# First expert layer: 320 slots per expert in blocks of 128, 128 and 64, where there were 336 in blocks of 128, 128 and 80

## The chip, the cores and the metric

The kernel runs on one core of a Trainium2 chip. The metric is the device time of one launch in microseconds (us). Engines are named as in the profile: PE (TensorE, matmuls), PEld (its weight loads), DVE (VectorE), ACT (ScalarE), POOL (GpSimd) and SP (SyncE, which here only issues transfers).

## The reference

Three layers stand behind each other: attention with a bias from running sums, a layer of eight experts with the two best per token, and a layer of eight experts in which every token goes to every expert. The first expert layer is the one that is changed:

```python
N, D, E, F = (1152, 512, 8, 1024)
logits = x @ w_gate
noisy_logits = logits + np.log1p(np.exp(x @ w_noise)) * noise
top2 = np.argpartition(-noisy_logits, 2, axis=1)[:, :2]
...
for e in range(E):
    for k in range(2):
        mask = top2[:, k] == e
        h = np.maximum(x[mask] @ w1[e], 0.0)
        out[mask] += top2_w[mask, k, None] * (h @ w2[e])
```

So 2304 pairs of token and expert are spread over eight experts, 288 for each on average. For the inputs of the reference its routing gives the experts 273, 287, 288, 283, 286, 286, 297 and 304 tokens.

## The kernel before

**Number format.** Values that go to PE are split in two fp16 parts, a high part and the rest (`hi`, `lo`; `hh`, `hl` for the hidden layer). A product is three matmuls: high by high, high by low, low by high.

**Order.** Each engine has its own queue, in order; the kernel schedules by hand, so the order of the code is the order of each queue. Steps on different engines wait for each other only through the data and buffers that they share.

**Attention** (to about 136 us) also issues, between its steps (`between`), work for what follows: the weights of the first expert (`w_load`) and `zero_rows`, which clears the first C0 rows of every expert's place in the DRAM tensor `xs_d`. There are two such transfers per expert, of C0/2 rows each, all from a small tile `z` of zeros, through SP's queue. SP's queue also carries the attention's loads, its transposes (`dma_start_transpose`) and a small transfer of row maxima per step (`rt` to `xq`, L246), for which PE waits in the next step.

**Routing** (`route`, `scatter`, `order`) finds the two best experts of each token, gives each token a slot in its experts, and writes the tokens' two parts to these slots of `xs_d` by indirect transfers of POOL (L826). The writes overlap the cleared rows, so they wait for the zeros. Expert 0's tokens are not read from DRAM: 72 matmuls with 0/1 matrices `hot0` of C0 columns select them (L971), and eight copies (L1011, L1013) put them in SBUF. Then comes a branch (L1016): if any expert has more than C0 tokens, `general()` computes the whole layer in fp32 for all tokens.

**First expert layer**, experts e = 0 to 7 one after the other. `fetch` brings the tokens of the next expert with a transposing transfer. For each of 8 slices f of the hidden layer there are 12 matmuls with C0 moving columns (L1051 to L1053); ACT makes the high part (L1054) and the full value in PSUM (L1055), and DVE subtracts (L1056). Then the slots go through w2 in blocks of up to 128 slots, which are the stationary side; the moving side has 512 columns. A block is 8 x 3 matmuls (L1070 to L1072); ACT copies the result out (L1074), and POOL, or SP for expert 7, issues its transfer to `y_d` (L1076). The weights of the next expert are split between these steps (`w_conv`): ACT makes the high part (L551), DVE the low part (L552), and then the next chunk is loaded into the buffer. Up to four chunks are in flight; from expert 7's weights on (`LAST`) two.

Beside expert 7, `lower` gathers each token's result of the lower of its two experts from `y_d` (L960, POOL) and adds it (L1026, DVE, one per slice f). After expert 7 the results of the other expert are gathered and added (L1125), and the sums, transposed on PE or by transfers (L1108), are the input of the second expert layer, which takes the rest of the time.

The block loop of the kernel before:

```python
BL = [(b, min(128, C0 - b)) for b in range(0, C0, 128)]
...
for b, n in BL:
    ps = bank()
    o = ps[0:n, :]
```

Of the kernel before, what the change touches and what calls it, by code (L numbers as in the profile page):

```python
# [438 lines left out]
SW1 = 16.0  # L439
SH2 = SX2 * SW1  # L440
CAP = 1152
C0 = 336
LAG = 2
NST = 2
NW = 8
# [10 lines left out]
def attention_moe_moe_kernel(  # L456
# [40 lines left out]
    def bank():  # L497
        return psum.tile([128, 512], F32, name="ps", tag="b")
# [156 lines left out]
    def zero_rows(i, z):  # L655
        if i == 0:
            nc.gpsimd.memset(z, 0.0)
        r0 = i // 2 * CAP + i % 2 * (C0 // 2)
        nc.sync.dma_start(out=xs_d[r0:r0 + C0 // 2, :].rearrange("(p r) (a c) -> p (r a) c", p=56, a=2),
                          in_=z.unsqueeze(1).to_broadcast([56, C0 // 56, D]))  # L660

    xhl_p = ctx.enter_context(tc.tile_pool(name="xhl", bufs=1))
    xall = xhl_p.tile([128, NT * 2 * D], F16, name="xall")
# [252 lines left out]
    with ExitStack() as actx:  # L916
        r_p = actx.enter_context(tc.tile_pool(name="r", bufs=1))

        z = r_p.tile([56, D], F16, name="z")

        gates_in = gate_weights()

        def between(it):
            if it == -4:
                constants()
            if 1 <= it < 7:
                next(gates_in)
            if it == 6:
                gate_split()
            if 12 <= it < 16:  # L930
                w_load(0, it - 11)
            if 8 <= it < 8 + E:
                zero_rows(2 * it - 16, z)
                zero_rows(2 * it - 15, z)
            if it == 9:
                first.append(route(r_p, 0, 4, False))
            if 13 <= it < 15:
                turn2(it - 13)
            if it == 16:
                gate_part()  # L940
                turn2(2)
            if it >= 9:
                next(first[0], None)

        attention(tc, actx, psum, q, k, v, s, xhl, scat, between, idle)
# [18 lines left out]
    with ExitStack() as m1:  # L964
# [69 lines left out]
        def fetch(e):  # L1034
            XT[e] = e_p.tile([128, 2 * KD, C0], F16, name="xsT")
            nc.sync.dma_start_transpose(out=XT[e], in_=xs_d[e * CAP:e * CAP + C0, :])

        BL = [(b, min(128, C0 - b)) for b in range(0, C0, 128)]
        for e in range(E):
            if 0 < e < E - 1:  # L1040
                fetch(e + 1)
            w_load(e + 1)
            xt = XT.pop(e)
            hh, hl = [e_p.tile([128, KF, C0], F16, name=f"h{u}") for u in "hl"]
            for f in range(KF):
                ps = bank()
                o = ps[:, 0:C0]
                fs = slice(f * 128, (f + 1) * 128)
                for c in range(KD):
                    wh, wl = [W[e, 0][u][:, c, fs] for u in range(2)]  # L1050
                    nc.tensor.matmul(out=o, lhsT=wh, rhs=xt[:, c, :], start=(c == 0), stop=False)  # L1051
                    nc.tensor.matmul(out=o, lhsT=wh, rhs=xt[:, KD + c, :], start=False, stop=False)  # L1052
                    nc.tensor.matmul(out=o, lhsT=wl, rhs=xt[:, c, :], start=False, stop=(c == KD - 1))  # L1053
                nc.scalar.activation(out=hh[:, f, :], in_=o, func=AF.Relu, scale=SH / (SX * SW))  # L1054
                nc.scalar.activation(out=o, in_=o, func=AF.Relu, scale=SH / (SX * SW))  # L1055
                nc.vector.tensor_tensor(out=hl[:, f, :], in0=o, in1=hh[:, f, :], op=OP.subtract)  # L1056
                if f % 2 or e == 0:
                    w_conv(e + 1)
                if e == 0 and f == FETCH:
                    fetch(1)  # L1060
                if e == E - 1:
                    next(lows)
            w2h, w2l = [t.rearrange("p c (a d) -> p (c a) d", a=2) for t in W[e, 1]]
            if e == E - 1:
                w_conv(E, False)
            for b, n in BL:
                ps = bank()
                o = ps[0:n, :]
                for f in range(KF):
                    nc.tensor.matmul(out=o, lhsT=hh[:, f, b:b + n], rhs=w2h[:, f, :], start=(f == 0), stop=False)  # L1070
                    nc.tensor.matmul(out=o, lhsT=hh[:, f, b:b + n], rhs=w2l[:, f, :], start=False, stop=False)  # L1071
                    nc.tensor.matmul(out=o, lhsT=hl[:, f, b:b + n], rhs=w2h[:, f, :], start=False, stop=(f == KF - 1))  # L1072
                y = e_p.tile([128, D], F32, name="y", bufs=3)
                nc.scalar.activation(out=y[0:n], in_=o, func=AF.Copy, scale=1.0 / (SH * SW))  # L1074
                eng = nc.gpsimd if e + 1 < E else nc.sync
                eng.dma_start(out=y_d[e * C0 + b:e * C0 + b + n, :], in_=y[0:n])  # L1076
                if e == E - 1 and b < 256:
                    ups.append(gather(b // 128, 1, e * C0 + b + 128))
                if e < E - 1 or b:
                    w_conv(e + 1, e + 1 < E)  # L1080
                next(lows, None)
            if e + 1 < E:
                w_conv(e + 1)
            if e == E - 2:
                lows = lower()
                next(lows)
# [340 lines left out]
```

## Time and profile before

| What | Value |
|---|---|
| median of 3 runs | 1158.96 us (1158.96 to 1161.39) |
| the profiled execution: time | 1163.45 us |
| the profiled execution: span | 1161.7 us |
| PE busy | 1086.6 us, 94% of the span |
| DVE, ACT, POOL busy | 51%, 43%, 21% |
| mean granted clock of PE | 0.968 of full speed |

The span runs from the first to the last instruction. Matmuls are pipelined: their "mean ns" is the time through the pipeline, so the cost of one is read from the distance between the starts of two. The granted clock is a share of full speed: 1.00 is 2.4 GHz, 0.50 is 1.2 GHz.

### The profile page before, as it was taken

What the parts mean: (1) busy time and instruction counts of PE and PEld (TensorE: products, weight loads), DVE (VectorE), ACT (ScalarE), POOL (GpSimd) and SP (SyncE); (2) the same over time, 40 slices, a digit from 0 to 9 for tenths busy, and PEclk for the clock granted to TensorE, in tenths of its full rate; (3) what the DMA queues carried; (4) which work ended last, traced back from release to release, by engine and by line L of the source; (5) the groups of instructions that cost most, each with busy time, mean ns of one, the idle gap of its engine ahead of it and who ended that gap; (6) DMA issues with size and microseconds to landing.
All of it is one profiled execution on the core that took longest, in us unless ns stands there. A gap on an engine that the chain in (4) does not pass through costs nothing.

```text
span 1161.7 us, 18353 instructions
## 1 busy us (share of the span) xinstructions
PE 1086.6 (94%) x7450; PEld 670.2 (58%) x7450; DVE 597.4 (51%) x1099; ACT 496.9 (43%) x926; POOL 242.9 (21%) x317
## 2 busy tenths in 40 slices
PE   4988739999999978999999999999999999999996
PEld 3566625555555557566666666566566566566553
DVE  8997745444444555755454444454454354354231
ACT  5786715555555433344443443343343343343220
POOL 6674570000000340441220220220220220220000
PEclk8798978999999998999999999999999999999998
DMA  5668666666654744021021021021021022010001
GB/s 99 126 119 153 201 219 178 202 190 191 191 191 155 223 125 128 19 73 55 19 73 55 19 73 55 19 73 56 19 71 58 19 64 65 19 55 1 10 28 46
DMA packets 134766, 108.41 MB, mean 93 GB/s; under 512 B 74546, under 2 KB 108642, under 8 KB 134674
## 3 DMA queue, kind: packets, MB, share of 16 engines
q1 hardware_dynamic: 130226, 92.90, 29.0%
q0 software_dynamic: 4448, 14.26, 3.5%
q8 instruction: 60, 0.98, 0.4%
q14 instruction: 32, 0.26, 0.1%
HBM read 79.03 MB, written 18.09 MB: 84 GB/s over the span
## 4 chain that ended last, share of the span: by engine, by line
PE 76%; DMA 2%; DVE 2%; issue 1%; ACT 1%; POOL 1%; SPq 0%; POOLq 0%; DVEq 0%; ACTq 0%
PE ps L1324 31%; PE ps L1266 24%; PE ps L1117 3%; PE ps L1071 3%; PE ps L1072 3%; PE ps L1070 3%; PE ps L1051 3%; PE ps L1052 3%; PE ps L1053 3%; DMA wst<-in_moe_w_dram 1%; DMA yg<-y_d,idy 1%; DVE wp L552 1%; ACT wp L551 1%; DVE hop L1238 0%; DMA y_d<-y 0%
## 5 line engine op out<-in xcount | busy, mean ns | idle before, releaser
L1324 PE MATMUL ps<-wp,hop 128*128 128x512 f16 x1536 | 366.6, 379 | 0.2 <-PE ps L1195 0.2
L1266 PEld LDWEIGHTS <-wp 128*128 128x128 f16 x2352 | 230.1, 98 | 101.2 <-issue 1.6
L1324 PEld LDWEIGHTS <-hop 128*128 128x128 f16 x1536 | 150.2, 98 | 141.6 <-issue 0.3
L552 DVE SCALAR_TENSOR_TENSOR wp<-wst,wp 128x1024 f16<-128x1024 f32 (+1 forms) x153 | 178.7, 1187 | 102.3 <-ACT wp L551 101.7
L1266 PE MATMUL ps<-xall,wp 128*128 128x256 f16 (+1 forms) x1344 | 192.1, 286 | 0.6 <-ACT z L1280 0.6
L551 ACT ACTIVATE wp<-wst 128x1024 f16<-128x1024 f32 (+1 forms) x153 | 150.9, 1008 | 10.0 <-DMA wst<-in_moe_w_dram 4.6
L1266 PE MATMUL ps<-xT,wp 128*128 128x256 f16 (+1 forms) x1008 | 150.9, 286 | 0.2 <-DVE z L1284 0.2
L562 POOL TENSOR_TENSOR wst<-wst 128x256 f32<-128x256 f32 x28 | 21.5, 769 | 440.8 <-DVE wp L552 440.8
L1284 DVE TENSOR_TENSOR z<-ps,z 128x256 f32<-128x256 f32 (+1 forms) x56 | 25.6, 458 | 137.7 <-ACT z L1283 137.7
L1301 DVE SCALAR_TENSOR_TENSOR acc<-ps,P,acc 128x512 f32<-128x512 f32 (+1 forms) x64 | 47.5, 742 | 94.6 <-PE ps L1324 94.6
L1051 PE MATMUL ps<-xsT,wp 128*128 128x336 f16 x256 | 79.6, 311 | 14.4 <-DVEq L1016 14.4
L1289 DVE TENSOR_TENSOR z<-ps,z 128x256 f32<-128x256 f32 (+1 forms) x56 | 25.7, 458 | 111.7 <-PE ps L1266 111.7
L1052 PE MATMUL ps<-xsT,wp 128*128 128x336 f16 x256 | 79.5, 311 | 0.0
L1053 PE MATMUL ps<-xsT,wp 128*128 128x336 f16 x256 | 79.4, 310 | 0.0
L1237 ACT ACTIVATE hop<-z 128x1024 f16<-128x1024 f32 x56 | 59.2, 1058 | 45.9 <-DVE z L1289 45.9
L1072 PE MATMUL ps<-wp,hl 128*128 128x512 f16 (+1 forms) x192 | 72.8, 379 | 1.7 <-DVE hl L1056 1.7
L1238 DVE SCALAR_TENSOR_TENSOR hop<-z,hop 128x1024 f16<-128x1024 f32 x56 | 68.1, 1216 | 11.1 <-ACT hop L1237 11.1
L1070 PE MATMUL ps<-wp,hh 128*128 128x512 f16 (+1 forms) x192 | 72.8, 379 | 0.5 <-ACT hh L1054 0.5
L1071 PE MATMUL ps<-wp,hh 128*128 128x512 f16 (+1 forms) x192 | 72.8, 379 | 0.0
L1280 ACT ACTIVATE z<-ps 128x256 f32<-128x256 f32 (+1 forms) x56 | 23.0, 411 | 108.1 <-PE ps L1266 108.1
L1287 ACT ACTIVATE z<-ps 128x256 f32<-128x256 f32 (+1 forms) x56 | 23.0, 411 | 99.7 <-PE ps L1266 99.7
L1283 ACT ACTIVATE z<-ps 128x256 f32<-128x256 f32 (+1 forms) x56 | 23.0, 411 | 96.3 <-PE ps L1266 96.2
(270 smaller groups left out, 1470.4 us busy)
## 6 DMA issues: line engine op xcount, KB each, us to landing
wst<-in_moe_w_dram SPq DMA_DIRECT2D x100, 512.0 KB
wst<-in_moe_w_dram SPq DMA_DIRECT2D x56, 256.0 KB
xs_d<-z SPq DMA_DIRECT2D x16, 336.0 KB
y_d<-y POOLq DMA_DIRECT2D x14, 256.0 KB
stq<-in_q_dram SPq DMA_DIRECT2D x8, 288.0 KB
stk<-in_k_dram SPq DMA_DIRECT2D x8, 288.0 KB
out_dram<-acc SPq DMA_DIRECT2D x9, 256.0 KB
stv<-in_v_dram SPq DMA_DIRECT2D x16, 128.0 KB
```

Source lines behind the costliest of these rows:

```text
L551: nc.scalar.activation(out=hi, in_=src, func=AF.Copy, scale=scale)
L552: run(todo, lambda: nc.vector.scalar_tensor_tensor(out=lo, in0=src, scalar=scale, in1=hi, op0=OP.mult, op1=OP.subtract))
L1051: nc.tensor.matmul(out=o, lhsT=wh, rhs=xt[:, c, :], start=(c == 0), stop=False)
L1052: nc.tensor.matmul(out=o, lhsT=wh, rhs=xt[:, KD + c, :], start=False, stop=False)
L1053: nc.tensor.matmul(out=o, lhsT=wl, rhs=xt[:, c, :], start=False, stop=(c == KD - 1))
L1070: nc.tensor.matmul(out=o, lhsT=hh[:, f, b:b + n], rhs=w2h[:, f, :], start=(f == 0), stop=False)
L1071: nc.tensor.matmul(out=o, lhsT=hh[:, f, b:b + n], rhs=w2l[:, f, :], start=False, stop=False)
L1072: nc.tensor.matmul(out=o, lhsT=hl[:, f, b:b + n], rhs=w2h[:, f, :], start=False, stop=(f == KF - 1))
L1237: nc.scalar.activation(out=hi, in_=x, func=AF.Relu)
L1238: nc.vector.scalar_tensor_tensor(out=lo, in0=x, scalar=0.0, in1=hi, op0=OP.max, op1=OP.subtract)
L1266: nc.tensor.matmul(out=o, lhsT=self.w[:, u, self.LEFT[m - 1], c * 128:(c + 1) * 128], rhs=x[h], start=start and c + u + h == 0, stop=c == ...
L1324: nc.tensor.matmul(out=ps, lhsT=x, rhs=w[h][:, f, d0:d0 + dn], start=(i + u + h == 0), stop=(i == KF - 1 and u == 1))
```

## The change

C0 becomes 320. Blocks are then 128, 128 and 64 slots. `hh` and `hl` become one tile `hp` with, for each slice f, the 320 high parts first, then the low parts of the last 64 slots, then those of the first 256. So the last 64 high parts and their low parts are 128 neighbouring columns, and one stationary operand holds both: times w2's high part it gives high by high in rows 0 to 63 and low by high in rows 64 to 127. The low part of w2 is multiplied by the same operand, so the low by low product comes along too. For the last block this is 8 x 2 matmuls; ACT copies out rows 64 to 127, and DVE adds rows 0 to 63 to them. DVE's subtraction is made in two parts, 64 and 256 columns. The tile of zeros has 40 partitions, where it had 56.

```diff
@@ -439,7 +439,7 @@
 SW1 = 16.0
 SH2 = SX2 * SW1
 CAP = 1152
-C0 = 336
+C0 = 320
 LAG = 2
 NST = 2
 NW = 8
@@ -656,8 +656,8 @@
         if i == 0:
             nc.gpsimd.memset(z, 0.0)
         r0 = i // 2 * CAP + i % 2 * (C0 // 2)
-        nc.sync.dma_start(out=xs_d[r0:r0 + C0 // 2, :].rearrange("(p r) (a c) -> p (r a) c", p=56, a=2),
-                          in_=z.unsqueeze(1).to_broadcast([56, C0 // 56, D]))
+        nc.sync.dma_start(out=xs_d[r0:r0 + C0 // 2, :].rearrange("(p r) (a c) -> p (r a) c", p=40, a=2),
+                          in_=z.unsqueeze(1).to_broadcast([40, C0 // 40, D]))
 
     xhl_p = ctx.enter_context(tc.tile_pool(name="xhl", bufs=1))
     xall = xhl_p.tile([128, NT * 2 * D], F16, name="xall")
@@ -916,7 +916,7 @@
     with ExitStack() as actx:
         r_p = actx.enter_context(tc.tile_pool(name="r", bufs=1))
 
-        z = r_p.tile([56, D], F16, name="z")
+        z = r_p.tile([40, D], F16, name="z")
 
         gates_in = gate_weights()
 
@@ -1035,13 +1035,20 @@
             XT[e] = e_p.tile([128, 2 * KD, C0], F16, name="xsT")
             nc.sync.dma_start_transpose(out=XT[e], in_=xs_d[e * CAP:e * CAP + C0, :])
 
+        CB = C0 - C0 % 128
+
+        def lower_at(c):
+
+            return C0 + (c - CB if c >= CB else c + C0 - CB)
+
         BL = [(b, min(128, C0 - b)) for b in range(0, C0, 128)]
         for e in range(E):
             if 0 < e < E - 1:
                 fetch(e + 1)
             w_load(e + 1)
             xt = XT.pop(e)
-            hh, hl = [e_p.tile([128, KF, C0], F16, name=f"h{u}") for u in "hl"]
+            hp = e_p.tile([128, KF, 2 * C0], F16, name="hp")
+            hh = hp[:, :, 0:C0]
             for f in range(KF):
                 ps = bank()
                 o = ps[:, 0:C0]
@@ -1053,7 +1060,10 @@
                     nc.tensor.matmul(out=o, lhsT=wl, rhs=xt[:, c, :], start=False, stop=(c == KD - 1))
                 nc.scalar.activation(out=hh[:, f, :], in_=o, func=AF.Relu, scale=SH / (SX * SW))
                 nc.scalar.activation(out=o, in_=o, func=AF.Relu, scale=SH / (SX * SW))
-                nc.vector.tensor_tensor(out=hl[:, f, :], in0=o, in1=hh[:, f, :], op=OP.subtract)
+
+                for a, b in ((CB, C0), (0, CB)):
+                    nc.vector.tensor_tensor(out=hp[:, f, lower_at(a):lower_at(a) + b - a], in0=o[:, a:b], in1=hh[:, f, a:b],
+                                            op=OP.subtract)
                 if f % 2 or e == 0:
                     w_conv(e + 1)
                 if e == 0 and f == FETCH:
@@ -1064,14 +1074,23 @@
             if e == E - 1:
                 w_conv(E, False)
             for b, n in BL:
-                ps = bank()
-                o = ps[0:n, :]
-                for f in range(KF):
-                    nc.tensor.matmul(out=o, lhsT=hh[:, f, b:b + n], rhs=w2h[:, f, :], start=(f == 0), stop=False)
-                    nc.tensor.matmul(out=o, lhsT=hh[:, f, b:b + n], rhs=w2l[:, f, :], start=False, stop=False)
-                    nc.tensor.matmul(out=o, lhsT=hl[:, f, b:b + n], rhs=w2h[:, f, :], start=False, stop=(f == KF - 1))
+                o = bank()
                 y = e_p.tile([128, D], F32, name="y", bufs=3)
-                nc.scalar.activation(out=y[0:n], in_=o, func=AF.Copy, scale=1.0 / (SH * SW))
+                if n == 128:
+                    for f in range(KF):
+                        nc.tensor.matmul(out=o, lhsT=hh[:, f, b:b + n], rhs=w2h[:, f, :], start=(f == 0), stop=False)
+                        nc.tensor.matmul(out=o, lhsT=hh[:, f, b:b + n], rhs=w2l[:, f, :], start=False, stop=False)
+                        nc.tensor.matmul(out=o, lhsT=hp[:, f, lower_at(b):lower_at(b) + n], rhs=w2h[:, f, :], start=False, stop=(f == KF - 1))
+                    nc.scalar.activation(out=y, in_=o, func=AF.Copy, scale=1.0 / (SH * SW))
+                else:
+
+                    for f in range(KF):
+                        x = hp[:, f, b:b + 2 * n]
+                        nc.tensor.matmul(out=o, lhsT=x, rhs=w2h[:, f, :], start=(f == 0), stop=False)
+                        nc.tensor.matmul(out=o, lhsT=x, rhs=w2l[:, f, :], start=False, stop=(f == KF - 1))
+                    nc.scalar.activation(out=y[0:n], in_=o[n:2 * n], func=AF.Copy, scale=1.0 / (SH * SW))
+                    nc.vector.scalar_tensor_tensor(out=y[0:n], in0=o[0:n], scalar=1.0 / (SH * SW), in1=y[0:n],
+                                                   op0=OP.mult, op1=OP.add)
                 eng = nc.gpsimd if e + 1 < E else nc.sync
                 eng.dma_start(out=y_d[e * C0 + b:e * C0 + b + n, :], in_=y[0:n])
                 if e == E - 1 and b < 256:
```

## Rows read from the trace of the kernel before

**Rows 1.** From the page: busy time of PE and PEld, and the zero transfers

```profile
PE 1086.6 (94%) x7450; PEld 670.2 (58%) x7450; DVE 597.4 (51%) x1099; ACT 496.9 (43%) x926; POOL 242.9 (21%) x317
...
xs_d<-z SPq DMA_DIRECT2D x16, 336.0 KB
```

**Rows 2.** Table of stretches: experts 1 and 6, most of 7; busy (instructions), clock, DMA

```profile
208.50:237.70 29.20, 29.20 (x169) 16.90 (x168) 13.32 (x16) 15.52 (x27) 1.66 (x3) 1.00 0.61 193
...
354.50:383.70 29.20, 29.20 (x170) 16.89 (x169) 13.33 (x16) 15.51 (x27) 1.64 (x3) 1.00 0.51 152
383.70:407.50 23.80, 21.63 (x132) 12.50 (x131) 15.37 (x22) 13.06 (x24) 10.86 (x10) 1.00 0.73 234
```

**Rows 3.** Timeline of expert 1: start, duration in us, engine, line

```profile
208.52 0.31 PE L1051 MATMUL ps<-xsT,wp 128*128 128x336 f16 x1
...
222.20 0.38 PE L1070 MATMUL ps<-wp,hh 128*128 128x512 f16 x1
...
222.41 0.38 PE L1071 MATMUL ps<-wp,hh 128*128 128x512 f16 x1
...
223.12 1.04 ACT L551 ACTIVATE wp<-wst 128x1024 f16<-128x1024 f32 x1
223.22 0.51 DVE L1056 TENSOR_TENSOR hl<-ps,hh 128x336 f16<-128x336 f32 x1 [0.81 <-ACT ps L1055]
```

**Rows 4.** Groups by line: count, busy us, mean ns, idle before

```profile
L1070 PE MATMUL ps<-wp,hh 128*80 128x512 f16 x64 | 24.3, 379 | 0.0
...
L1056 DVE TENSOR_TENSOR hl<-ps,hh 128x336 f16<-128x336 f32 x64 | 31.7, 503 | 22.7 <-ACT ps L1055 22.7
...
L1026 DVE SCALAR_TENSOR_TENSOR acc<-yg,gates,acc 128x512 f32<-128x512 f32 x9 | 6.7, 746 | 4.6 <-DMA yg<-y_d,idy 4.6
...
L1238 DVE SCALAR_TENSOR_TENSOR hop<-ps,hop 128x256 f16<-128x256 f32 x32 | 13.1, 421 | 18.4 <-ACT hop L1237 18.3
...
L1238 DVE SCALAR_TENSOR_TENSOR h<-ps,h 128x64 f16<-128x64 f32 x16 | 3.6, 225 | 4.7 <-ACT h L1237 4.7
```

**Rows 5.** Timeline from the end of expert 6 into expert 7

```profile
384.04 0.59 ACT L1074 ACTIVATE y<-ps 80x512 f32<-80x512 f32 x1 [3.64 <-PE ps L1072]
...
388.35 1.03 POOL L960 DMA_INDIRECT yg<-y_d,idy  x1 [2.89 <-DVE wp L552]
...
392.96 0.75 DVE L1026 SCALAR_TENSOR_TENSOR acc<-yg,gates,acc 128x512 f32<-128x512 f32 x1 [4.57 <-DMA yg<-y_d,idy]
...
404.09 0.39 PE L1072 MATMUL ps<-wp,hl 128*128 128x512 f16 x1 [1.40 <-DVE hl L1056]
```

**Rows 6.** Timeline from the end of expert 7 to the second layer

```profile
415.95 0.59 ACT L1074 ACTIVATE y<-ps 80x512 f32<-80x512 f32 x1 [3.64 <-PE ps L1072]
...
419.78 1.40 POOL L960 DMA_INDIRECT yg<-y_d,idy  x1 [4.13 <-DVE xall L1105]
...
438.63 0.38 PE L1164 MATMUL ps<-wg,xall 128*128 128x16 f16 x8 [7.00 <-DMA xall<-x]
```

**Rows 7.** Table of stretches in the attention; the last two columns are DMA share and GB/s

```profile
87.00:89.00 2.00, 2.00 (x18) 1.17 (x16) 2.00 (x4) 2.00 (x5) 0.96 (x2) 1.00 0.86 207
95.00:96.00 1.00, 1.00 (x24) 0.85 (x25) 1.00 (x3) 0.53 (x2) 1.00 (x1) 1.00 0.02 4
118.00:138.00 20.00, 15.46 (x267) 12.57 (x265) 15.80 (x54) 13.83 (x38) 9.44 (x16) 0.91 0.85 246
```

**Rows 8.** Timeline from the attention's last steps to expert 0

```profile
120.56 0.70 SPq L246 DMA_DIRECT2D xq<-rt  x1
...
125.81 0.19 PE L260 MATMUL ps<-xq,xk 69*64 69x64 f16 x1 [2.30 <-DMA xq<-rt]
...
140.98 1.28 POOL L826 DMA_INDIRECT xs_d<-xall,idx  x1 [0.26 <-DVE u L773]
...
169.30 0.96 POOL L826 DMA_INDIRECT xs_d<-xall,idx  x1 [0.21 <-issue]
...
176.65 0.44 PE L1051 MATMUL ps<-xsT,wp 128*128 128x336 f16 x1 [14.36 <-DVEq L1016]
```

## The prediction

> **What bounds the kernel now.** I read the page first [rows 1]: TensorE (PE) is busy for 94% of the span, so where PE has no gap, columns removed from it should come back as time. That is an average, so I cut the span at the stages. First-layer experts run from 176.6 to about 416 us. In the table of stretches [rows 2] the reader is to see that a middle expert takes 29.20 us with PE busy for all of it at granted clock 1.00 (the 2.4 GHz level), while VectorE (DVE) and ScalarE (ACT) are busy for half and the DMA engines for some 0.6. So experts 0 to 6 are bound by PE alone. The last expert is another matter: in its stretch PE is busy for 21.63 of 23.80 us.
>
> Then the timeline of one expert [rows 3]. From the first w1 matmul (208.52) to the first w2 matmul (222.20) there are 96 instructions, so 0.1425 us each for 336 columns; one w2 matmul of 512 columns takes 0.215 us (222.20 to 222.41). The "mean ns" of the groups (379) is the time through a pipeline and not the spacing. The slope is (0.215 - 0.1425) / 176 = 0.41 ns a column.
>
> **The change, part by part.**
>
> *Fewer columns in w1.* 96 matmuls an expert lose 16 columns each: 96 x 16 x 0.41 ns = 0.63 us.
>
> *The last block.* It goes from 24 matmuls with 80 slots as the stationary side (L1070 with 128*80) [rows 4] to 16 with 128, all of 512 moving columns. They show the same 379 ns as the 128-wide ones of rows 3 (0.38 us), so the count decides: 8 x 0.215 = 1.72 us. Together 2.35 us an expert, 16.5 us for experts 0 to 6. The first one starts with some 5 us at the lower clock; these pass in either kernel.
>
> *Subtraction in two parts.* L1056 takes 503 ns for 336 columns. The nearest rows for its parts are L1238's, 421 ns for 256 and 225 for 64 [rows 4]: at most 0.15 us more each time, 1.2 us an expert. DVE has 13.3 us of work in 29.2 [rows 2], so for experts 0 to 6 it costs nothing. Without that cover it would cost 8 x 1.2 = 9.6 us. ACT's 16 columns fewer give nothing either, since ACT waits for PE.
>
> *Eviction of the last block.* ACT's copy (0.59 us) stays, and a DVE instruction over 512 columns comes behind it: 0.75 us by L1026 [rows 4], with the hand-over some 0.8. The output transfer waits for it. Queued behind it on DVE are the low parts of the two weight chunks at the expert's end, whose high parts ACT makes only after its copy, 1.04 us each [rows 3]; 0.75 us fits ahead of them, so experts 0 to 5 pay nothing. The store shrinks from 160 to 128 KB, which I take as nothing.
>
> *The last expert.* The gathers of expert outputs (L960) can begin only when expert 6's last block is in DRAM: eviction at 384.04, first gather at 388.35, first use on DVE at 392.96 [rows 5]. DVE is in order: weight chunks and L1056 stand behind that use, ACT's next weight chunk needs a buffer that these free, and PE stalls for about 2.2 us in the first output block (the one at 404.09 stands for three). This chain starts at expert 6's eviction, whatever PE does. It gets 0.8 us longer by the new instruction, and 0.2 us by the two-part subtractions. PE's 0.63 us in w1 then only waits longer. What is left behind the stall is one block: 1.72 - 1.0 = 0.7 us for expert 7. (If the stall had another cause, 2.35 or nothing; both stay in the range.)
>
> *The turn to the second layer.* The last block is evicted at 415.95, the first gather that needs it starts at 419.78, six more follow it, and PE takes up again at 438.63 after transposes of what they brought [rows 6]. All is one chain, so the new instruction costs 0.75 us here.
>
> *The zero rows.* The easily missed part. Sixteen transfers of 336 KB [rows 1] clear the slots in DRAM, in pairs on SP's queue during the attention. The tile is now 40 partitions high, not 56. While such a pair is alone in flight, the mean busy share of the 16 DMA engines stands at 0.86 with 207 GB/s (87 to 89 us) [rows 7]. That is 14/16, and 56 = 14 x 4: the partitions seem to be dealt out in equal whole numbers, so two engines get none. 40 dealt so goes to 10 engines (10 x 4), which gives 207 x 10/14 = 148 GB/s. A pair of 672 KB takes 688 kB / 207 = 3.3 us, the new one of 640 KB 655 kB / 148 = 4.4 us: 1.1 us longer, on ten engines. The Trainium skill says the same of this ("DMA: Bandwidth & Descriptors", section "Why a DMA increments its semaphore by 16 and not by 1"): the number of engines is the largest up to 16 that divides the slowest dimension of both sides. By that rule it would be 14 before and 10 after; the trace agrees with the first. If instead the tile went to all 16, the new pair would take 655 / (207 x 16/14) = 2.8 us and the term were nil or a small gain.
>
> Is this on the path? From 118 to 138 us the DMA engines are busy at 0.85 on average [rows 7], with 14 of them near full: four weight chunks and four pairs of zeros go through. The attention's last transfer of row maxima (issued 120.56) [rows 8] stands behind a pair, and PE waits 2.30 us for it at 125.81: that wait grows by one pair's 1.1 us, or by 2.2 if the pair before is late too; I take 1.5. The scatter at 140.98 may not begin before all zeros have landed. They end at about 138.5 (the share falls off behind 138); four pairs make that 138.5 + 4.4 = 142.9, and with a completion of some 0.6 it is 143.5, 2.5 us after the scatter starts now. From there GpSimd (POOL) runs without a gap to its last scatter at 169.30, and the first expert starts at 176.65. So I take 2.5 us for this (it holds the 1.5, which delay the same chain). Bounds: 0, if the copies and the branch ahead of the first expert hide it (ACT and DVE wait there for something that the trace does not name), and 8 pairs x 1.1 = 8.8, if each pair delays the chain.
>
> *Nothing* for the 72 selection matmuls and 8 copies with 16 columns fewer ahead of the first expert: they run beside the scatters, which end later (169.30).
>
> **Sum:** 16.5 + 0.7 - 0.75 - 2.5 = 14.0 us (13.95). The profiled execution is 1163.45 us (span 1161.7), so it would be 1149.4 profiled. The three unprofiled runs have the median 1158.96; less 14.0, that is 1145.0.
>
> **Rivals.**
>
> 1. *The zeros cost nothing*, spread over all engines or hidden at the branch: gain 16.5, 1142.5. For it: the unnamed wait ahead of the first expert. Against: the 0.86 of rows 7, and PE's wait at 125.81 [rows 8].
> 2. *All eight pairs stand on the path*: gain 16.45 - 8.8 = 7.7, 1151.3. Against: between the pairs up to 115 us the DMA engines have idle stretches (0.02 from 95 to 96 us) [rows 7], where a late pair is made up for.
> 3. *The shared tile makes w2 wait.* High and low parts of h now lie in one tile. If w2's first matmul waited for the whole tile, PE would wait from 222.20 to the end of the last L1056 at 223.73 [rows 3], and with two parts some 1.6 us, 8 x 1.6 = 12.8 us: gain 1.2, 1157.8, no change. Against: in rows 3 w2 starts while the last row of the same tile hh is not yet written, so waits go by rows and not by tiles.
> 4. *Weight feeding becomes the bound* in expert 6, which has only two chunks in flight: it would keep its 29.2 us, gain 11.6, 1147.3. Against: a DMA share of 0.51 and half-idle ACT and DVE [rows 2].
> 5. *Slower: the fallback runs.* If an expert gets more than C0 tokens, a branch computes the layer in fp32, with the weights read anew for each of three token groups: 3 x 33.5 MB at the 246 GB/s of rows 7 is 409 us, so 1550 or more. It decides from 321 tokens on. The reference's routing gives 273 to 304 per expert for its inputs, so this needs other inputs.
>
> **How the numbers follow.** Forecast 0.58; rivals 0.17, 0.12, 0.04, 0.06 and 0.03 in their order. Below 0.2% (2.3 us) a measurement of this kernel can hardly tell a difference from none. Forecast and rivals 1, 2 and 4 are faster: 0.93; rival 3 is the same: 0.04; rival 5 slower: 0.03. The range takes in rival 1 (1142.5) with the last expert's whole 2.35 us (1140.9), so 1141, and upwards rival 4 and about half of rival 2, a loss of 7 us at the zeros, 1149.5. What lies above, the rest of rival 2, rivals 3 and 5, and what lies below come to 2 in 10.
>
> **What would show it.** Middle experts of 26.85 us with PE busy throughout; the w1 spacing at 0.136 us; 16 matmuls in the last block. Zero transfers alone in flight at share 0.62 and 148 GB/s; the last of PE's waits for a row transfer at 3.4 us or more; the first scatter and the first expert's start 2 to 3 us later (at about 179). From expert 6's last eviction to expert 7's 31.2 us, against 415.95 - 384.04 = 31.9. The seven gathers some 0.75 us later after PE's last matmul. The prediction is wrong if middle experts stay above 28 us, if PE waits at the start of w2, or if the first expert starts on time or over 5 us late.

## The result and the profile after

The changed kernel takes 1141.32 us (median of 6 runs, 1137.29 to 1155.34) against 1160.44 us for the kernel before beside it on the same chip: ratio 0.9829, 95% interval 0.9805 to 0.9854. One of the six, 1155.34, is a disturbed execution; without it the median is 1140.3. So the change gained about 20 us where 14.0 were forecast, and the time lies 0.7 us below the forecast's low end of 1141. Two later timings of the same kernel gave 1141.07 and 1138.72 us.

The page of the changed kernel, first the busy time of the engines, then the zero transfers:

```profile
PE 1073.3 (94%) x7386; PEld 663.2 (58%) x7386; DVE 605.7 (53%) x1171; ACT 494.3 (43%) x926; POOL 242.1 (21%) x317
...
xs_d<-z SPq DMA_DIRECT2D x16, 320.0 KB
```

64 matmuls and 13.3 us of PE's busy time are gone [rows 1], but the span is 21.1 us shorter: part of the gain is time in which PE waited. I cut both profiled executions (1163.45 before, 1142.3 after) at the evictions of the experts' last blocks (those of expert 0 are shown below) and at the first matmul that the second layer has to wait for:

| stretch | before | after | difference |
|---|---|---|---|
| to the end of expert 0 | 208.72 | 204.84 | -3.9 |
| experts 1 to 6 | 175.32 | 161.12 | -14.2 |
| expert 7 | 31.92 | 29.79 | -2.1 |
| turn to the second layer | 22.67 | 22.82 | +0.15 |
| from there on | 723.1 | 722.0 | -1.1 |

The last stretch took 721.8 to 723.1 us in executions of both kernels, so its 1.1 us are not put down to the change.

The table of stretches of the changed kernel, with columns as in rows 2 (the last two are DMA share and GB/s): two stretches in which a pair of zero transfers is nearly alone in flight, then expert 2.

```profile
111.00:112.00 1.00, 1.00 (x4) 0.41 (x3) 0.00 (x0) 0.93 (x4) 0.65 (x1) 0.50 0.64 201
121.00:124.00 3.00, 3.00 (x63) 2.43 (x61) 1.47 (x3) 2.89 (x6) 0.27 (x1) 1.00 0.66 186
231.70:258.50 26.80, 26.80 (x162) 15.61 (x161) 14.39 (x25) 15.23 (x27) 1.66 (x3) 1.00 0.69 206
```

The reader is to see two things. An expert takes 26.85 us (161.12 / 6) and PE is busy in all of it, as before at 29.20 [rows 2]. And the zeros' DMA share fell from 0.86 [rows 7] to 0.64 and 0.66, near 10/16. The rate did not fall with it: 201 GB/s in the first of these stretches, against 207 before and 148 forecast.

The groups by line, shapes apart (count, busy us, mean ns, idle before):

```profile
L1090 PE MATMUL ps<-wp,hp 128*128 128x512 f16 x64 | 24.3, 379 | 0.0
...
L1065 DVE TENSOR_TENSOR hp<-ps,hp 128x256 f16<-128x256 f32 x64 | 26.6, 415 | 0.0
L1065 DVE TENSOR_TENSOR hp<-ps,hp 128x64 f16<-128x64 f32 x64 | 14.1, 220 | 25.2 <-ACT ps L1062 16.5 <-PE ps L1060 8.7
L1092 DVE SCALAR_TENSOR_TENSOR y<-ps,y 64x512 f32<-64x512 f32 x8 | 5.5, 683 | 10.2 <-ACT y L1091 10.2
```

A matmul of the last block with 128 stationary columns takes the 379 ns that it took with 80 [rows 4]; the parts of the subtraction take 415 and 220 ns (421 and 225 were assumed), the added VectorE instruction 0.68 (0.75).

The end of expert 0 in the kernel before, then the timeline of the changed kernel from the zeros' landing to the end of expert 0 and from expert 6's end to the second layer (start, duration, in brackets the engine's wait and what ended it; of every timeline here only chosen lines are shown):

```profile
208.72 0.59 ACT L1074 ACTIVATE y<-ps 80x512 f32<-80x512 f32 x1 [3.64 <-PE ps L1072]
```

```profile
150.56 1.06 ACT L586 ACTIVATE wp<-wst 128x1024 f16<-128x1024 f32 x1 [3.02 <-DMA xs_d<-z]
151.43 1.22 POOL L826 DMA_INDIRECT xs_d<-xall,idx  x1 [2.86 <-DVE i L793]
152.84 8.06 PE L971 MATMUL ps<-hot,xall 128*128 128x320 f16 x56
154.08 1.18 DVE L909 TENSOR_SCALAR hot<-iotac,low 128x320 f16<-128x320 f16 x5
156.51 6.29 POOL L588 TENSOR_TENSOR wp<-wst,wp 128x1024 f16<-128x1024 f32 x3
156.91 5.92 DVE L848 TENSOR_SCALAR dn<-dg 128x9 f32<-128x9 f32 x1 [0.95 <-ACT wst L587]
171.31 0.42 PE L1058 MATMUL ps<-xsT,wp 128*128 128x320 f16 x1 [10.41 <-DMA wst<-in_moe_w_dram]
...
182.97 0.44 ACT L1061 ACTIVATE hp<-ps 128x320 f16<-128x320 f32 x1 [6.10 <-remote]
...
204.84 0.59 ACT L1091 ACTIVATE y<-ps 64x512 f32<-64x512 f32 x1 [1.91 <-PE ps L1090]
...
365.96 0.59 ACT L1091 ACTIVATE y<-ps 64x512 f32<-64x512 f32 x1 [1.91 <-PE ps L1090]
370.71 1.11 POOL L960 DMA_INDIRECT yg<-y_d,idy  x1 [2.60 <-DMA y_d<-y]
374.91 0.75 DVE L1026 SCALAR_TENSOR_TENSOR acc<-yg,gates,acc 128x512 f32<-128x512 f32 x1 [3.53 <-DMA yg<-y_d,idy]
385.56 0.39 PE L1083 MATMUL ps<-wp,hp 128*128 128x512 f16 x1 [1.46 <-DVE hp L1065]
...
395.75 0.59 ACT L1091 ACTIVATE y<-ps 64x512 f32<-64x512 f32 x1 [1.91 <-PE ps L1090]
...
418.57 0.38 PE L1183 MATMUL ps<-wg,xall 128*128 128x16 f16 x8 [5.66 <-DMA xall<-x]
```

The first scatter starts at 151.43, 10.5 us later than before [rows 8], and yet expert 0 starts 5.3 us earlier. That contradiction is what most experiments were for. Some 3 us of the delay were there before the first zero transfer (87.61 against 84.60), and a later execution of the changed kernel lacks them (84.95, with the first scatter at 148.79); 7 to 8 us are the zeros'.

### The profile page after: what moved, and what is told of

Read it like the earlier page. It is cut to its first block, busy times and chain, and to the rows that moved or that the text cites. A ratio compares the mean times of both kernels' runs of the same rounds, so it can differ in the third digit from the quotient of the medians.

```text
span 1140.6 us, 18334 instructions
## 1 busy us (share of the span) xinstructions
PE 1073.3 (94%) x7386; PEld 663.2 (58%) x7386; DVE 605.7 (53%) x1171; ACT 494.3 (43%) x926; POOL 242.1 (21%) x317
## 4 chain that ended last, share of the span: by engine, by line
PE 82%; DVE 7%; ACT 3%; DMA 2%; issue 2%; SPq 2%; POOL 1%; DVEq 0%; POOLq 0%; ACTq 0%
PE ps L1343 32%; PE ps L1285 25%; PE ps L1136 3%; PE ps L1058 3%; PE ps L1060 3%; PE ps L1059 3%; PE ps L1083 2%; PE ps L1082 2%; PE ps L1081 2%; DVE mx L226 1%; PE ps L1090 1%; PE ps L1089 1%; DMA wst<-in_moe_w_dram 1%; PE ps L212 1%; DVE el L271 1%
## 5 line engine op out<-in xcount | busy, mean ns | idle before, releaser
L1285 PE MATMUL ps<-xall,wp 128*128 128x256 f16 (+1 forms) x1344 | 192.1, 286 | 0.6 <-ACT z L1299 0.6
L1058 PE MATMUL ps<-xsT,wp 128*128 128x320 f16 x256 | 78.4, 306 | 10.8 <-DMA wst<-in_moe_w_dram 10.4
L1060 PE MATMUL ps<-xsT,wp 128*128 128x320 f16 x256 | 78.4, 306 | 0.8 <-issue 0.8
L1059 PE MATMUL ps<-xsT,wp 128*128 128x320 f16 x256 | 78.4, 306 | 0.4 <-issue 0.4
L1136 PE MATMUL ps<-xall,wp 128*128 128x256 f16 (+1 forms) x384 | 51.1, 291 | 0.4 <-DVE xall L1124 0.4
L1083 PE MATMUL ps<-wp,hp 128*128 128x512 f16 x128 | 48.6, 379 | 2.1 <-DVE hp L1065 1.8
L1095 POOL DMA_DIRECT2D y_d<-y x21 | 11.7, 557 | 174.9 <-ACT y L1084 149.6
```

Of the source, the lines that this page charges most:

```text
L1083: nc.tensor.matmul(out=o, lhsT=hp[:, f, lower_at(b):lower_at(b) + n], rhs=w2h[:, f, :], start=False, stop=(f == KF - 1))
L1136: nc.tensor.matmul(out=ps[:, s0:s1], lhsT=W[E, 0][u][:, c, f * 128:(f + 1) * 128], rhs=x2T[:, h * KD + c, c0 + s0:c0 + s1], start=(c + u + ...
L1285: nc.tensor.matmul(out=o, lhsT=self.w[:, u, self.LEFT[m - 1], c * 128:(c + 1) * 128], rhs=x[h], start=start and c + u + h == 0, stop=c == ...
```

## The experiments

The runs fell on several chips. The kernel before takes some 1150 us on two of them (12 and 14) and some 1160 on the others (6, 11 and that of the result). So times are compared with those taken beside them on the same chip. The ratio to the kernel before carries over between the two kinds of chip only in part: the kernel before itself spends its 10 us more ahead of expert 0, in the stretch in question (expert 0 ends at 208.72 us on the chip of the result and at 198.00 on chip 12). The changed kernel itself was not timed on a chip of 1150 us, only variants of it.

**Is the first layer's gain PE's alone?** The changed kernel with the last block of 64 as three groups of matmuls again (the edit also lets these matmuls and their copy take 64 rows; that part is not shown):

```
-                if n == 128:
+                if n == 128 or e >= 0:
```

> The changed kernel, but the block of 64 slots is computed as the other blocks are: 24 matmuls and no addition on DVE behind the copy. The count of matmuls decides: 8 x 8 x 0.215 = 13.8 us more PE work; a middle expert takes 28.6 us instead of 26.86. Theory A, that the added instruction costs nothing on the two chains at the end: 1140.3 + 13.8 = 1154 us. Theory B, that it costs 0.75 us at the turn to the second layer and about 1 us in expert 7: 1152.4 us.

Ratio 1.0002 (0.9983 to 1.0022), on chip 14; the stretch of expert 2:

```profile
228.50:257.30 28.80, 28.80 (x170) 16.57 (x169) 13.71 (x24) 15.13 (x27) 1.65 (x3) 1.00 0.65 192
```

28.80 us an expert: 1.95 of the 2.35 us come from the block, 0.40 from the 16 columns of w1 (1.72 and 0.63 were forecast). That all of the gain is gone, although w1 keeps its 0.40 us an expert, says that something else in this run is late. The profile shows where: expert 0 starts at 171.58, 5.9 us later than in an execution of the kernel before on chip 12 (165.69). The runs on the zeros below tell why.

The same in expert 7 alone (`if n == 128 or e == E - 1`):

> The changed kernel, but for expert 7 alone the block of 64 slots takes 24 matmuls and no addition on DVE. If the addition lies on the chain to the second layer (0.75 us), the stretch from the last eviction's start to the second layer's first matmul falls from 22.82 to about 22.1 us and the kernel takes 1.72 - 0.75 = 1.0 us more. If the gathers behind it hide the addition, that stretch stays at 22.7 to 22.9 us and the kernel takes 1.7 us more.

Ratio 0.9875 (0.9853 to 0.9897), on chip 14 too. From expert 6's end to expert 7's 31.4 us, against 29.4 to 31.3 in most executions with the new block; the turn took 20.9 us, against 22.7 to 23.4. The two about cancel. That the ratio is higher than the changed kernel's 0.983 has another cause, which the account below comes to.

**The added instruction at the turn.** It is left out in the last expert:

```
+                    if e + 1 < E:
                         nc.vector.scalar_tensor_tensor(out=y[0:n], in0=o[0:n], ...
```

> The changed kernel without the added VectorE instruction in the last expert alone (its last 64 slots keep one of the two parts). If that instruction stands on the chain of the turn to the second layer, the stretch from the last block's eviction to the second layer's first matmul falls from 22.8 by 0.7 to 1.3 us, ratio some 0.001 below that of the changed kernel. If the chain hides it, nothing.

> The kernel before once more, for its stages in another execution: ratio 1.000. If its 22.7 us from the last block's eviction to the second layer was one execution's, it comes out at 21 to 22 us, as in other kernels without the added instruction; if the added instruction costs nothing there, at 22.7 again.

Without the instruction the turn takes 23.16 us, in the second execution of the kernel before 23.03. The first gather that needs the last block, in the timeline of the run without the instruction (with it, the eviction is at 395.75 and the gather at 400.49):

```profile
392.53 0.94 POOL L960 DMA_INDIRECT yg<-y_d,idy  x1 [1.99 <-DMA y_d<-y]
...
411.97 0.38 PE L1184 MATMUL ps<-wg,xall 128*128 128x16 f16 x8 [5.54 <-DMA xall<-x]
```

The eviction stood at 388.81, so the gather comes after 3.72 us, and after 4.74 with the instruction. It does delay the gathers as forecast, but in this execution the turn is not shorter without it. The ratio, 0.9849 (0.9827 to 0.9872), can't tell, as the changed kernel was not timed on this chip (12); the kernel before gave 1.0006 (0.9984 to 1.0028).

**The zeros' engines, with nothing else changed.** The zero tile 80 partitions high in the changed kernel; and 24 high, so 12 engines, in the kernel before (one of two changed places is shown, the other is the tile itself):

```
-  ..."(p r) (a c) -> p (r a) c", p=40, a=2), in_=z.unsqueeze(1).to_broadcast([40, C0 // 40, D])
+  ..."(p r) (a c) -> p (r a) c", p=80, a=2), in_=z.unsqueeze(1).to_broadcast([80, C0 // 80, D])
```

> The changed kernel, with the tile of zeros 80 partitions high (16 x 5) instead of 40 (10 x 4); the same bytes. Theory A, that the zeros on ten engines delay the attention and through it the first expert: a pair alone in flight shows a DMA share near 1.00, the attention ends some 5 us earlier than with 40, expert 0 starts some 3 to 5 us earlier, and the kernel takes about 1136 to 1138 us. Theory B, that what the zeros cost is taken up by the wait ahead of expert 0, where in the kernel before PE was idle for 14.4 us: the attention still ends 5 us earlier, but expert 0 starts within 1.5 us of where it did, and the time stays at 1140 to 1142 us, or is longer if that wait comes back.

> The kernel before, with the tile of zeros 24 partitions high (12 x 2) instead of 56 (14 x 4); the same bytes. If the partitions are dealt out in equal whole numbers, a pair alone in flight shows a share of 0.75. Theory A: eight pairs of 3.85 us instead of 3.3 delay the attention by 2 to 4 us and the kernel by about as much, 1162 to 1165 us. Theory B: the attention's end moves by 2 to 4 us, the first expert's start does not follow it, and the time is 1160 us or less; the idle stretch of PE ahead of expert 0 gets shorter than 14.4 us.

Ratios 0.9832 (0.9809 to 0.9855) and 1.0017 (1.0001 to 1.0034), both on chip 14. Then both widths side by side on a chip of 1160 us (6):

> The changed kernel unaltered, beside the three others on one chip. The kernel before takes about 1150 us on a second chip and 1160 on the first, so the sum is tried here again. If the sum of the prediction holds (16.5 + 0.7 - 0.75 - 2.5), the gain is 14 us, ratio 0.988. If the part ahead of expert 0 costs nothing, the gain is 16.5, ratio 0.9855. If the first result holds everywhere, it is 20 us, ratio 0.983.

> The changed kernel with the tile of zeros on 16 engines, beside the unaltered one on the same chip. Theory A (the zeros on ten engines delay expert 0): 2 to 4 us less than the unaltered changed kernel. Theory B (taken up ahead of expert 0): within 1 us of it.

0.9823 (0.9798 to 0.9849; 1141.07 us) with 10 engines, 0.9833 (0.9807 to 0.9859; 1141.43) with 16. The stretch with a pair alone in the run with 80 partitions shows the full share:

```profile
87.00:89.00 2.00, 1.56 (x12) 0.83 (x11) 2.00 (x4) 1.33 (x3) 1.67 (x3) 1.00 0.95 239
```

So the faster zeros are there, the first scatter starts at 139.75 and not at 151.54 (2.8 us of that stood before the first zeros), and on this chip the kernel gains nothing by it: expert 0 ends at 204.11 and 204.77. On chip 14 it is different. The run with 16 engines took 1131.31 us there, the one with 10 engines and the old block in expert 7 took 1136.77; of these 5.5 us the block explains 1.95 at most, so some 3.5 are the zeros'. In the kernel before, 12 engines instead of 14 cost about 2 us. The term has no fixed size; something between the zeros and expert 0 decides.

**Is it the branch?** The fallback branch left out, in both kernels:

```
-        with tc.If(nc.values_load(cmx[0:1, 0:1]) > C0):
-            general()
```

> The kernel before without the branch to the fp32 fallback; the fallback for more than C0 tokens is left out, and with it the meeting of all engines at the branch. Theory: the wait ahead of expert 0 is the branch (each engine loads a count, jumps, and waits for the semaphores of the others). Then expert 0 starts within 1 us of the last of the eight copies of its tokens, and the kernel takes 4 to 8 us less. Rival: expert 0 waits for its weights or for the scatters anyway; then it starts as late as with the branch, and the time is the same within 1 us.

> The changed kernel without the branch; the fallback is left out. If the branch hides what the zeros cost, the gain against the same kernel before is smaller here than with the branch: 16.5 + 0.7 - 0.75 less some 3 to 5 us for the later end of the attention, so 11.5 to 13.5 us. If it hides nothing, the two gains agree within 1 us.

0.9963 (0.9947 to 0.998) and 0.979 (0.9748 to 0.9831): the branch costs 3.9 us in the kernel before and 5 to 6 in the changed one, whose times without it spread over 16 us. Between the two kernels lie 20 to 21 us without the branch and 19.3 with it. It is not what hides the zeros.

**More zeros' time, or no scatters.** A tile of 5 partitions; and the changed kernel without `scatter(2, NT)`:

> The changed kernel with the zeros' tile 5 partitions high, so by the dealing-out on 5 engines instead of 10: a pair alone in flight should show a DMA share of 0.31 and take some 8.9 us instead of 4.4. If the wait ahead of expert 0 swallows what the zeros delay, the last attention steps come some 10 to 20 us later than with 10 engines, the ratio stays near 0.983 until that cover (the 14.4 us PE idle ahead of expert 0 before) is used up, so 0.983 to 0.990. If each pair's extra time stands on the path as the prediction had it for its last pairs (2.5 us for 1.1 us a pair), 4.5 us more a pair make 10 us, ratio 0.992; if all eight pairs stand there, 36 us, ratio 1.014.

> The changed kernel without the 14 scatters behind the first 4 (the rows of experts 1 to 7 that they carry stay zero). If the scatters' traffic or their issue by GpSimd holds the start of expert 0 back, PE's idle stretch and the interrupted matmuls there go: expert 0 ends some 8 to 12 us earlier, ratio 0.972 to 0.976. If the wait belongs to the copies, the branch or the instructions of the next stage, expert 0 ends as before this edit, within 2 us, ratio 0.981 to 0.985.

With 5 engines the ratio is 1.1018 (1.0997 to 1.1038), far beyond every expectation. A stretch of it, then its timeline from the landing of the last zeros:

```profile
120.00:140.00 20.00, 2.27 (x37) 2.00 (x35) 2.73 (x13) 0.39 (x2) 0.67 (x1) 0.50 0.31 48
```

```profile
281.09 1.06 ACT L586 ACTIVATE wp<-wst 128x1024 f16<-128x1024 f32 x1 [52.95 <-DMA xs_d<-z]
287.00 6.27 POOL L588 TENSOR_TENSOR wp<-wst,wp 128x1024 f16<-128x1024 f32 x3
287.43 5.87 DVE L848 TENSOR_SCALAR dn<-dg 128x9 f32<-128x9 f32 x1 [50.91 <-ACT dg L839]
299.81 0.43 PE L1058 MATMUL ps<-xsT,wp 128*128 128x320 f16 x1 [58.35 <-DVEq L1016]
```

The share is 5/16 as forecast, but a pair takes 22.4 us from its first packet to its last, where 8.9 were expected. The run lays the chain bare: ScalarE's weight conversions wait for the zeros, GpSimd's subtractions (L588) follow, VectorE stands still meanwhile, and 18.7 us after the zeros' landing expert 0 starts. In the changed kernel it is 20.75 us from the first conversion to expert 0 (150.56 to 171.31), in its other executions 18.9 and 19.8, and in the kernel before 37.0 and 26.3. So after the change expert 0 does hang on the zeros, and before it on something that comes later.

Without the scatters nothing is gained: 0.9884 (0.9854 to 0.9915), expert 0 starts at 173.03. On this chip (12) their traffic is not what holds expert 0.

**The stall on VectorE.** L848 handles 9 columns a partition and takes 0.35 us or less where L588 does not run; beside L588 it takes 5.9. The timeline of the kernel before in its second execution shows where this stall fell there:

```profile
145.22 0.24 DVE L815 TENSOR_TENSOR hot<-hot,rk 128x80 f32<-128x80 f32 x1
145.76 6.45 DVE L818 CAST idx<-slot 128x10 int32<-128x10 f32 x1
145.90 6.27 POOL L588 TENSOR_TENSOR wp<-wst,wp 128x1024 f16<-128x1024 f32 x3
152.31 1.29 DVE L909 TENSOR_SCALAR hot<-iotac,low 128x336 f16<-128x336 f16 x5
152.70 9.00 PE L971 MATMUL ps<-hot,xall 128*128 128x336 f16 x44 [6.02 <-DVE hot L909]
165.69 0.44 PE L1051 MATMUL ps<-xsT,wp 128*128 128x336 f16 x1 [3.99 <-DVEq L1016]
```

Here it falls *ahead* of L909, which makes the last five selection matrices, and PE waits 6.02 us for them. In the profiled execution of the changed kernel the late zeros hold back ScalarE's conversions and the four scatters that stand ahead of L588 on GpSimd, L588 starts at 156.51, and the stall falls *behind* L909 (154.08): the 56 selection matmuls run through in 8.06 us, and what stands still is the ordering of the gates (`order`). With 16 engines it lies ahead again, in the timeline of the second run with 80 partitions:

```profile
145.75 5.42 DVE L815 TENSOR_TENSOR hot<-hot,rk 128x80 f32<-128x80 f32 x1
...
151.75 1.38 DVE L909 TENSOR_SCALAR hot<-iotac,low 128x320 f16<-128x320 f16 x5
...
152.33 7.61 PE L971 MATMUL ps<-hot,xall 128*128 128x320 f16 x44 [6.70 <-DVE hot L909]
```

The margin is small. Of the kernels with the branch and zeros on 10 engines, five profiled executions have the stall behind L909 and two ahead of it: the changed kernel with the old block in all experts and the one without scatters. There late zeros and stall are both paid. With 12 engines in the kernel before it takes in L909 itself (7.85 us). If this order is what pays for late zeros, then zeros must count again once the stall is gone. Three kernels have three chunks of expert 0's weights split by ScalarE and VectorE behind the matrices, where ScalarE and GpSimd split them ahead of them:

```
-        for _ in range(3):
-            w_conv(0, pool=True)
 ...
         hots(4, NT)
+        for _ in range(3):
+            w_conv(0)
         order(r_p)
```

> The kernel before with its three weight chunks split by ScalarE and VectorE behind the selection matrices, instead of ScalarE and GpSimd ahead of them. If GpSimd's subtractions hold VectorE up there, no VectorE instruction of some 5 to 6 us is left between 140 and 160 us, the last selection matmul comes some 4 to 6 us sooner after the first scatter (20.6 us before), and the kernel gets 2 to 5 us faster, ratio 0.996 to 0.998. If the stall has another cause, VectorE only has 3.7 us more to do ahead of expert 0: no change or up to 3 us slower, 1.000 to 1.003.

> The same edit in the changed kernel, zeros on 10 engines. If the swap is right, there is nothing to win at the selection matrices, as the block lies behind them already, only the shorter chain from the zeros' landing to expert 0 (three times 1.04 and 1.23 us in place of three times 2.1 and a block of 6.3): 0 to 5 us, ratio to the changed kernel 0.996 to 1.000.

> The same edit in the changed kernel with zeros on 16 engines. If the swap is right, the early end of the attention now reaches expert 0: 2 to 5 us faster than the changed kernel, and not slower than the run with the edit and 10 engines. If the zeros have no hold on expert 0 at all, the same as that run.

> The changed kernel itself, beside the three others: ratio 0.982 to 0.984 if the zeros cost nothing, 0.985 to 0.987 where the zeros' 2.5 us are paid.

Side by side, on a chip of 1160 us (11):

| kernel | us | ratio to the kernel before |
|---|---|---|
| before, edit | 1155.79 | 0.9949 (0.9924 to 0.9975) |
| changed | 1138.72 | 0.9825 (0.9809 to 0.984) |
| changed, edit | 1138.54 | 0.9804 (0.9784 to 0.9824) |
| changed, 16 engines, edit | 1129.58 | 0.9729 (0.9712 to 0.9747) |

With GpSimd's subtractions in place, 16 engines instead of 10 were worth -0.4 us on chip 6 (1141.07 to 1141.43); with them gone, 9.0 us on chip 11. In the profiled pair of the latter 4.4 us of it are there at the start of expert 0 (168.66 and 164.26) and 5.9 at its end. The timeline of the fastest:

```profile
148.65 1.29 DVE L909 TENSOR_SCALAR hot<-iotac,low 128x320 f16<-128x320 f16 x5
149.00 8.22 PE L971 MATMUL ps<-hot,xall 128*128 128x320 f16 x44 [2.81 <-DVE hot L909]
149.85 3.48 DVE L552 SCALAR_TENSOR_TENSOR wp<-wst,wp 128x1024 f16<-128x1024 f32 x3
164.26 0.43 PE L1058 MATMUL ps<-xsT,wp 128*128 128x320 f16 x1 [7.04 <-SPq L1016]
```

PE's wait for the matrices is down from 6.7 to 2.8 us, and expert 0 ends at 192.65, against 199.85 in the changed kernel beside it. The expectation for this kernel (2 to 5 us) was too low, and in the kernel before the last selection matmul came only 1.9 us sooner after the first scatter (18.7 against 20.6), less than the 4 to 6 expected, though its time fell by 4.4.

## Why the prediction missed

By stages, the profiled pair puts most of the miss ahead of expert 1. To the end of expert 0 the forecast has 2.5 - 2.35 = 0.15 us more, and it was 3.9 us less. For experts 1 to 6 it has 14.1 us less (14.2 came), for expert 7 0.7 less (2.1), for the turn 0.75 more (0.15), and for the rest nothing (1.1 less).

*Experts 0 to 6: right.* 161.12 against 175.32 us for six experts is 2.37 us each, forecast 2.35. The inner split was off by some 0.25 us (1.95 for the block and 0.40 for w1, by the run with the old block); the sum was not. The subtraction in two parts is hidden. PE does not wait at the start of w2 (rival 3 falls), and expert 6 takes no longer than the others (rival 4 falls).

*The zero rows: this step failed.* The first half held: the zeros go to 10 engines, as the rule of the Trainium skill has it ("DMA: Bandwidth & Descriptors", section "Why a DMA increments its semaphore by 16 and not by 1"), with shares of 0.64, 0.95 and 0.31 for 40, 80 and 5 partitions. A pair got 1.2 us longer (the first one, from its first packet to its last: 4.1 us before, 5.3 after), as forecast (1.1), though not by a rate of 148 GB/s: the zeros move at some 200 GB/s for 2.6 us, and the rest at some 50. The delay was even larger than the 2.5 us, some 8 at the first scatter, as rival 2 had it for eight pairs.

The wrong step is "From there GpSimd (POOL) runs without a gap to its last scatter at 169.30, and the first expert starts at 176.65. So I take 2.5 us for this". Expert 0 does not start after the last scatter; in the changed kernel it starts at 171.31 while scatters run until 180. It starts after the selection matmuls and the copies, and these stood behind VectorE's stall. The late zeros pushed the stall behind the matrices, and what they cost came back there: from the first scatter to the last selection matmul it takes 9.1 to 9.8 us in the three executions of the changed kernel, and 19.9 to 21.0 in those of all kernels with the stall ahead. The bound of 0 "if the copies and the branch ahead of the first expert hide it" was in the text, but not with its mechanism; it needed the one long VectorE instruction between 145 and 153 us, which the forecast did not look for.

How much is left of the delay differs between the two kinds of chip. On those of 1150 us expert 0 starts 24.4 to 25.2 us after the first scatter where the stall lies ahead of L909 or on it (five executions, the kernel before among them), and 17.7 us after it in the run without the added instruction, where the stall lies behind. So the 8.2 us of later scatter cost 1.0 us there. In the run with the old block in expert 7 the stall lies behind L909 too, but ahead of another VectorE instruction (L842) that PE needs:

```profile
159.66 5.09 PE L971 MATMUL ps<-hot,xall 128*128 128x320 f16 x24 [4.56 <-DVE cf L842]
```

There expert 0 starts 4.6 us later than in the kernel before. These two runs gained 16.8 and 13.9 us over the kernel before beside them, near the forecast's 14.0. On these chips the 2.5 us were too coarse, but not far off, and that is luck: their reason was wrong.

On the chips of 1160 us a second wait comes in. The kernel before on the chip of the result:

```profile
165.47 0.45 ACT L1013 ACTIVATE xsT<-ps 128x336 f16<-128x336 f32 x1 [6.97 <-remote]
172.61 0.45 ACT L1013 ACTIVATE xsT<-ps 128x336 f16<-128x336 f32 x1 [6.69 <-remote]
```

ScalarE's last copies wait for counts from PE that come 7 us apart, though the matmuls are recorded done by 162 (their ends are modelled); "remote" says that the trace has no instruction that ends where the count comes. With the same first scatter (140.98 and 140.78) expert 0 starts at 176.65 here and at 165.69 on chip 12, where no such wait is seen. The run with 80 partitions on chip 6 shows the same. In the changed kernel the copies are through earlier, and the wait (6.10 us, shown above) falls inside expert 0, which takes 32.1 to 35.2 us here and 28.8 and 29.9 in the two variants on chips 12 and 14. So the kernel before loses some 11 us to it and the changed kernel some 2 to 6. That is read from single executions and no run tests it, but it is of the size of what the change gained above the forecast. *What holds the counts stays open.* It is not the branch, since the waits are there without it. The scatters remain a suspect: in all nine executions with such waits the last one ends 0.9 to 3.2 us after the last scatter starts, and the run without scatters fell on a chip that does not show them.

So the table of the last four runs is not the whole answer. With the stall away, 10 engines cost 9.0 us (and the profile with 16 shows no second wait, the one with 10 engines one of 2.55 us); with it there they cost nothing on chip 6, where the run with 16 engines also had the second wait ahead of expert 0, and some 3.5 us on chip 14. That the order of stall and matrices pays for late zeros is shown; that it alone makes them free is not.

*The last expert: a term too small.* 0.7 us was forecast, 2.1 came in the profiled pair. Over ten executions with the new block in expert 7 the stretch takes 30.5 us on average (29.4 to 32.5), over five of the kernel before and its variants 31.6 (31.0 to 32.6): 1.1. The first use of a gather comes 8.95 us after expert 6's eviction, against 8.92 before [rows 5]: store and gather took up the added instruction, so the stall did not get longer as assumed.

*The turn to the second layer: forecast 0.75, not settled.* The gathers that need the last block do start 0.7 to 1.0 us later. Over nine executions with the added instruction the turn takes 23.0 us on average (22.7 to 23.4), over the five of the kernel before and its variants 22.0 (21.3 to 23.0): 1.0 us, in line with the forecast. But the one run that leaves out the instruction alone has 23.2. Together with expert 7 the two terms come to 0.1 us on average, where the forecast had -0.05.

Without the 2.5 us, with 7 x 2.37 = 16.6 for PE, 1.1 for expert 7 and 1.0 lost at the turn the sum is 16.7 us, of about 20 measured; rival 1 (1142.5, zeros that cost nothing) came nearest, for a reason that it did not name. The rest is of the kind of the second wait, and its cause is open.

## What to carry to other kernels

A delay is priced along the chain that it lengthens, so the chain has to be followed to the instruction that starts late, and not to the last one of its kind (here the scatters). An instruction that takes many times what its shape needs (here 5.9 us instead of 0.35 or less) is a wait in disguise: look at what the other engine is doing in that time, and ask whether the change moves it ahead of or behind the work that counts. When a suspected cost measures nothing, remove what may cover it and measure again: that turned -0.4 into 9.0 us, and gave a kernel 9.1 us faster than the changed one. And a ratio to the kernel before carries over to another chip only if the kernel before waits at the same places there; its profiles on the two kinds of chip showed that it does not.

## What the hardware showed that was not expected

While GpSimd ran three subtractions of 128 x 1024 (6.27 us together), the VectorE instruction that met them stood still for nearly all of it: 5.3 to 7.1 us for instructions that otherwise take 0.2 to 1.3. With the subtractions moved to VectorE no such stall is left. The Trainium skill has the rule ("SBUF — State Buffer", section "Who interferes with whom"): the two engines share a pair of ports as an exclusive lock, and where VectorE works in a mode with two ports, whoever issues first holds the pair for the whole instruction and the other is fully blocked. The trace agrees that one is blocked, and shows that back-to-back GpSimd instructions kept VectorE out through all three. Who came first it does not show: in the second execution of the kernel before the VectorE instruction is recorded 0.14 us ahead of GpSimd's first (145.76 and 145.90) and still ends with its last.

Fewer DMA engines cost more than in proportion. From its first packet to its last, the first pair of zeros takes 3.1 us on 16 engines, 5.3 on 10 and 22.4 on 5, for the same bytes. With 5 engines all transfers together moved 48 GB/s from 120 to 140 us, and the kernel took 1266.65 us against 1149.93 for the kernel before: the attention's small transfers stand in the same queue, and from 100 to 110 us no engine worked at all, at a DMA share of 0.35.
